# Thresholded attention and a gMLP on one core: the threshold taken as a sign bit on GpSimd and VectorE, one Exp per step, and q, k transposed by half tiles

## The chip, the cores and the metric

The kernel runs on one core of one Trainium2 chip. The metric is the device time of one execution in microseconds. The kernel before took 428.83 us, the median of three runs (428.46 to 429.54).

## The reference, cut to what matters

```python
scale = 1.0 / np.sqrt(64)                       # q, k, v: (8, 8, 576, 64)
scores = scale * (q @ k.T)
thresh = max(scores, axis=-1) - tau             # tau = 0.02
scores = where(scores >= thresh, scores, -1e9)
attn = softmax(scores)
x = (attn @ v) in the layout (8, 576, 512)      # heads side by side
h = relu(x @ w_in); u, v = halves of h          # w_in: 512 x 1024
v_n = layernorm(v)
v_s = w_spatial @ v_n + b_spatial               # w_spatial: 576 x 576
out = (u * v_s) @ w_out                         # w_out: 512 x 512
```

So every query row keeps only the keys whose score lies within tau of the row's largest, and a gated MLP follows for each of the 8 batches.

## The kernel before, in words

The attention is cut into 144 steps, 18 for each batch. A step `g` holds 128 queries of two heads of one pair against all 576 keys. These pieces belong to a step, each named by a letter in the order lists:

- `S`, `G`, `Y` (`scores`, `turn_bank`, `scores_end`, line 830): TensorE computes both heads' scores in fp32 into one of two PSUM rings `s`, in four 64x64 quarters of the array. `G` is an empty instruction on another engine that orders two writes to one bank.
- `M` (`top`, line 859): VectorE copies each head's 128x576 scores from PSUM to SBUF (`e`, a ring of 3) and finds the row maximum `peak` on the way. TensorE may write that `s` ring again only when `M` is done.
- `B` (`shift`, lines 869 and 873): 128x2 elements, `negm` from `peak`, on VectorE or GpSimd.
- `E`, `F` (`spread`, lines 887 and 890): ScalarE, once for each head. In the steps that the table `WAYS` marks `a` it is a Prelu with slope 1e30 below the threshold, and `Z` (`exps`, line 925) is then one Exp over both heads, 128x1152. In the 42 steps marked `n` it is an Exp to fp16, and VectorE then makes a mask (`C`, `keep`, line 909) and ands it in (`A`, `pick`, line 918).
- `T` (`turn_p`) transposes the numerators `p` by DMA into `pT`, and `P`, `i`, `p` (`product`) multiply them with v and normalise.

Besides, each pair of heads has its q and k transposed on TensorE. `QA` and `QB` (`qk_main`, line 448) are one block for q and one for k, four fp32 transposes of 128x128 each into one PSUM bank `f`, and `qa`, `qb` evict one bank each on ScalarE or VectorE (`evict`, lines 422 to 430); q is multiplied by the scale there. Two `f` banks serve all products and transposes that aren't scores.

The order of all work on every engine is written out by hand: `ORDER` has one list of tokens for each batch, `run_token` calls the piece that a token names, and each engine works through its own queue in that order. A `d` ahead of a token moves its eviction to VectorE; `a`, `g`, `v` ahead of `G` or `B` name the engine.

Of the kernel before, what the change touches and what calls it, by code (L numbers as in the profile page):

```python
# [34 lines left out]
(  # L35
# [18 lines left out]
(  # L54
# [117 lines left out]
(  # L172
# [1090 lines left out]
```

## Time and profile before

| | |
|---|---|
| median of the runs | 428.83 us |
| profiled execution, its own time | 429.39 us |
| its span | 427.6 us |
| busy: PE, DVE, ACT, POOL | 405.0, 384.0, 386.1, 191.4 us |
| TensorE clock | granted in full in all of the span |

PE is TensorE, DVE is VectorE, ACT is ScalarE, POOL is GpSimd. Busy time counts an engine's instructions from start to end, where two overlap once. A matmul's recorded end is modelled, so a busy PE isn't PE at its peak. Around the span lie 1.8 us of the profiled execution's own time, and the median is 0.6 us under that time.

### The profile page before, as it was taken

What the parts mean: (1) busy time and instruction counts of PE and PEld (TensorE: products, weight loads), DVE (VectorE), ACT (ScalarE), POOL (GpSimd) and SP (SyncE); (2) the same over time, 40 slices, a digit from 0 to 9 for tenths busy, and PEclk for the clock granted to TensorE, in tenths of its full rate; (3) what the DMA queues carried; (4) which work ended last, traced back from release to release, by engine and by line L of the source; (5) the groups of instructions that cost most, each with busy time, mean ns of one, the idle gap of its engine ahead of it and who ended that gap; (6) DMA issues with size and microseconds to landing.
All of it is one profiled execution on the core that took longest, in us unless ns stands there. A gap on an engine that the chain in (4) does not pass through costs nothing.

```text
span 427.6 us, 13266 instructions
## 1 busy us (share of the span) xinstructions
PE 405.0 (95%) x4978; PEld 253.3 (59%) x5029; DVE 384.0 (90%) x1035; ACT 386.1 (90%) x567; POOL 191.4 (45%) x469
## 2 busy tenths in 40 slices
PE   8778978999999999999999999999999999999995
PEld 4456655566555675575665657656665666565642
DVE  6999989999899899989999999989999989999562
ACT  4999979999999999999999999999999999999362
POOL 2566437763246633554235631374233753255020
PEclk9999999999999999999999999999999999999999
DMA  7999999999999999998999989999989999989913
GB/s 196 288 280 182 263 273 227 168 182 195 239 265 171 214 213 188 204 210 227 214 165 280 211 165 252 217 221 210 236 138 229 228 214 206 160 150 214 180 57 117
DMA packets 224703, 88.18 MB, mean 206 GB/s; under 512 B 195648, under 2 KB 220352, under 8 KB 224640
## 3 DMA queue, kind: packets, MB, share of 16 engines
q1 hardware_dynamic: 224192, 86.75, 102.3%
q8 instruction: 39, 0.64, 0.6%
q10 hardware_dynamic: 368, 0.33, 0.2%
q0 software_dynamic: 80, 0.26, 0.2%
q14 instruction: 24, 0.20, 0.2%
HBM read 32.79 MB, written 9.44 MB: 99 GB/s over the span
## 4 chain that ended last, share of the span: by engine, by line
PE 62%; DVE 11%; ACT 9%; DMA 7%; issue 5%; POOL 3%; SPq 1%; POOLq 0%; DVEq 0%; ACTq 0%
PE s L830 25%; DVE e L859 7%; PE f L752 6%; DMA pT<-p 6%; PE f L448 5%; PE f L510 5%; PE f L723 4%; PE f L656 4%; ACT e L890 3%; PE f L781 3%; ACT e L887 2%; PE f L505 2%; ACT p L925 1%; DMA xT<-xn 1%; PE f L641 1%
## 5 line engine op out<-in xcount | busy, mean ns | idle before, releaser
L859 DVE CUSTOM_DVE_ANT_0 e<-s,zero 128x576 f32<-128x576 f32 x288 | 204.3, 752 | 5.8 <-PE s L830 1.4
L830 PE MATMUL s<-qkT 64*64 64x160 f32 (+1 forms) x2304 | 172.9, 413 | 4.5 <-DVE peak L859 3.7
L890 ACT ACTIVATE e<-e,negm 128x576 f32<-128x576 f32 x204 | 148.3, 766 | 4.8 <-PE s L830 2.3
L830 PEld LDWEIGHTS s<-qkT 64*64 64x64 f32 x2304 | 105.3, 132 | 53.2 <-issue 19.1
L925 ACT ACTIVATE p<-e 128x1152 f16<-128x1152 f32 x102 | 117.1, 1157 | 0.8
L873 POOL TENSOR_SCALAR negm<-peak 128x2 f32<-128x2 f32 x93 | 21.5, 231 | 133.3 <-DVE peak L859 89.7
L887 ACT ACTIVATE e<-e,negm 128x576 f16<-128x576 f32 x84 | 62.4, 767 | 2.0 <-POOL negm L873 1.3
L510 PE MATMUL f<-v,pT 128*128 128x65 bf16 x984 | 44.6, 194 | 0.0
L510 PEld LDWEIGHTS <-pT 128*128 128x128 f16 x1024 | 41.9, 98 | 2.4 <-issue 0.6
L918 DVE TENSOR_TENSOR p<-e 128x576 int32<-128x576 int32 x42 | 34.4, 822 | 0.5
L752 PE MATMUL f<-wsT,vn 128*128 128x512 bf16 x121 | 31.9, 380 | 0.9 <-DVE qkT L424 0.2
L505 PE MATMUL f<-v,pT 128*128 128x130 bf16 x123 | 27.2, 221 | 4.0 <-DMA pT<-p 3.9
L333 POOL CAST v<-vl 128x512 bf16<-128x512 f32 x32 | 21.3, 666 | 18.6 <-PE s L830 17.5
L708 POOL TENSOR_SCALAR vn<-vrel,rs,nm 128x512 bf16<-128x512 f32 (+1 forms) x35 | 27.9, 798 | 3.6
L723 PE MATMUL f<-xT,w_in 128*128 128x512 bf16 x102 | 28.5, 380 | 1.0 <-ACT qkT L430 0.3
L656 PE MATMUL f<-w_in,xT 128*128 128x512 bf16 x98 | 27.0, 380 | 1.4 <-DMA xT<-xn 0.3
L548 DVE TENSOR_TENSOR xn<-f,r 128x384 bf16<-128x384 f32 x46 | 25.2, 554 | 0.7
L781 PE MATMUL f<-w_o,gT 128*128 128x512 bf16 x94 | 25.1, 379 | 0.4
L859 DVE DVE_READ_ACCUMULATOR2_ANT peak<- 128x1 f32 x288 | 23.9, 83 | 0.0
L306 POOL COPY qn<-ql 128x512 f32<-128x512 f32 x31 | 19.7, 636 | 5.9 <-DMA ql<-in_q_dram 2.7
L752 PEld LDWEIGHTS <-vn 128*128 128x128 bf16 x140 | 12.8, 98 | 15.5 <-issue 3.1
L448 PE MATMUL f<-identf,kn 128*128 128x128 f32 x124 | 19.8, 282 | 2.2 <-DVE qkT L424 1.5
(175 smaller groups left out, 560.2 us busy)
## 6 DMA issues: line engine op xcount, KB each, us to landing
vl<-in_v_dram SPq DMA_DIRECT2D x16, 512.0 KB, 5.2
ql<-in_q_dram SPq DMA_DIRECT2D x15, 512.0 KB, 5.5
kl<-in_k_dram SPq DMA_DIRECT2D x15, 512.0 KB, 5.7
out_dram<-oo SPq DMA_DIRECT2D x12, 512.0 KB, 4.2
pT<-p SPq DMA_TRANSPOSE x141, 4.4
uT<-in_moe_w_in_dram SPq DMA_DIRECT2D x3, 512.0 KB, 6.4
uT<-in_moe_w_spatial_dram SPq DMA_DIRECT2D x2, 576.0 KB, 6.8
vx<-in_v_dram SPq DMA_DIRECT2D x16, 64.0 KB, 3.8
```

The source lines that it names most:

```text
L448: nc.tensor.transpose(out=t[:, c * P:(c + 1) * P], in_=nat[i][which][:, c, :], identity=identf)
L505: nc.tensor.matmul(out=t[:, at:at + 130], lhsT=pt[:, 4, rows], rhs=vt[:, 4:6, :].rearrange("p b d -> p (b d)"), start=True, stop=False)
L510: nc.tensor.matmul(out=t[:, at + 65 * h:at + 65 * h + 65], lhsT=pt[:, 5 * h + j, rows], rhs=vt[:, 6 * h + j, :], start=False, stop=(h == 1 ...
L656: nc.tensor.matmul(out=t, lhsT=x_of(b, f, slice(c * P, (c + 1) * P)), rhs=w_in[:, f, 512:1024], start=(f == 0), stop=(f == 3))
L723: nc.tensor.matmul(out=t, lhsT=w_in[:, m, f * P:(f + 1) * P], rhs=x_of(b, m, slice(0, 512)), start=(m == 0), stop=(m == 3))
L752: nc.tensor.matmul(out=t, lhsT=vn[:, c, f * P:(f + 1) * P], rhs=wsT[:, c, 0:512], start=(c == 0), stop=(c == 4))
L781: nc.tensor.matmul(out=t[:n], lhsT=gs[b][:, f, c * P:c * P + n], rhs=w_o[:, f, :], start=(f == 0), stop=(f == 3))
L830: made.append(nc.tensor.matmul(out=s_ring[g % 2][halves[k], at[h] + lo:at[h] + hi], lhsT=qks[n][halves[h], 0, m:m + 64], rhs=qks[n][halves ...
L859: nc.vector.tensor_tensor_reduce(out=e_ring[g % 3][:, h, :], in0=view(s_ring[g % 2], at[h], [[1, S]]), in1=zero.broadcast_to([P, S]), scal ...
L887: nc.scalar.activation(out=half_e(g)[0][:, h, :], in_=s, func=ACT.Exp, bias=bias_, scale=scale if steps[g][1] == 4 else 1.0)
L890: nc.scalar.activation(out=e, in_=s, func=ACT.Prelu, bias=bias_, scale=scale if steps[g][1] == 4 else 1.0, alpha=1e30)
L925: nc.scalar.activation(out=numerators(g), in_=e_ring[g % 3].rearrange("p h s -> p (h s)"), func=ACT.Exp)
```

## The change: what it does

- **The threshold.** `M` now multiplies by the scale as it copies. `B` (`bound`) makes `low = tau - peak`. `E` and `F` (`spread`) are one add and one multiply, `(s + low) * 2^-126`, in place in `e`, for all 288 heads of steps: a kept score becomes a small positive fp32 whose bits, read as an int32, are `(s - peak + tau) * 2^23`, and every other one is negative and so a hugely negative int32. `Z` is one Exp over 128x1152 for every step, which reads `e` as int32, multiplies by 2^-23 and adds -tau. The ways, the masks and the `C`, `A` tokens are gone.
- **Where it runs.** `E` and `F` leave ScalarE: 154 of the 288 are on GpSimd and 134 on VectorE (the `d` tokens). `B` is 71 times on GpSimd and 73 times on VectorE, before 93 and 51. `Z` on ScalarE is 144 instead of 102.
- **q and k.** `QX` transposes q and k of a pair in one block of 16 transposes: each reads 64 rows of the array and writes 128x64, and they go in turn to the two halves of the rows and to the two `f` banks. `qx` and `qy` each evict a whole bank, with half of the columns of q and of k. The scale isn't applied there any more.
- **Rings.** `e` has 4 buffers instead of 3, `p` 9 instead of 10.
- **Lists.** All order lists are new. Evictions moved with them: of the 62 of q and k 8 are on VectorE (before 27) and 54 on ScalarE (before 35), and VectorE has 8 fewer of the 128x512 evictions of `uT` (11 before).

```diff
-    def qk_main(i, which):
+    def qk_main(i):
+        hold = []
         def mm():
-            t = hold["t"] = bank()
-            for c in range(4):
-                nc.tensor.transpose(out=t[:, c * P:(c + 1) * P], in_=nat[i][which][:, c, :],
-                                    identity=identf)
+            hold.extend(bank() for _ in range(2))
+            for c in range(8):
+                w, n = divmod(c, 4)
+                for r in range(2):
+                    nc.tensor.transpose(
+                        out=hold[r][:, 64 * c:64 * c + 64], in_=nat[i][w][halves[r], n, :],
+                        identity=identf[halves[r], halves[r]])
+        def ev(r):
+            dst = qk_of(i)[:, :, 64:S].rearrange("p w (c s) -> p w c s", c=4)
+            evict(dst[:, :, :, 64 * r:64 * r + 64],
+                  hold[r].rearrange("p (w c s) -> p w c s", w=2, c=4))
...
-                in1=zero.broadcast_to([P, S]), scale=1.0, scalar=float("-inf"),
+                in1=zero.broadcast_to([P, S]), scale=scale, scalar=float("-inf"),
...
+    def bound(g):
+        low[g] = small.tile([P, 2], F32, name="low")
+        (nc.vector if on_vector[0] else nc.gpsimd).tensor_scalar(
+            out=low[g], in0=peak[g], scalar1=-1.0, scalar2=tau, op0=ALU.mult, op1=ALU.add)
     def spread(g, h):
-        if way(g) in "nrs":
-            nc.scalar.activation(out=half_e(g)[0][:, h, :], in_=s, func=ACT.Exp,
-                                 bias=bias_, scale=scale if steps[g][1] == 4 else 1.0)
-        elif on_act(g):
-            nc.scalar.activation(out=e, in_=s, func=ACT.Prelu, bias=bias_,
-                                 scale=scale if steps[g][1] == 4 else 1.0, alpha=1e30)
+        e = e_ring[g % NE][:, h, :]
+        (nc.vector if on_vector[0] else nc.gpsimd).tensor_scalar(
+            out=e, in0=e, scalar1=low[g][:, h:h + 1], scalar2=2.0 ** (SHIFT - 149),
+            op0=ALU.add, op1=ALU.mult)
-    def keep(g):
...
-    def pick(g):
...
     def exps(g):
-        nc.scalar.activation(out=numerators(g), in_=e_ring[g % 3].rearrange("p h s -> p (h s)"),
-                             func=ACT.Exp)
+        nc.scalar.activation(out=numerators(g),
+                             in_=e_ring[g % NE].rearrange("p h s -> p (h s)").bitcast(I32),
+                             func=ACT.Exp, bias=wrap, scale=2.0 ** -SHIFT)
```

The rows below are the engines' queues in the order of the program. On VectorE, between the tops of steps 87 and 88 (batch 4), before:

```order
L545 RECIPROCAL r<-f_92 128x6
L548 TENSOR_TENSOR xn<-f_92,r 128x384
L909 TENSOR_SCALAR e_109<-e_109 128x2x576
L859 ISA e_108,peak<-s_96,zero 128x576
L859 ISA peak 128x1
L859 ISA e_108,peak<-s_96,zero 128x576
L859 ISA peak 128x1
L869 SCALAR_TENSOR_TENSOR negm<-peak,raised 128x2
L918 TENSOR_TENSOR p_116<-e_109 128x576
```

And after the change, at the same place (`e_106` to `e_109` are the four buffers of `e`):

```order
L848 TENSOR_SCALAR low<-peak 128x2 x2
L854 TENSOR_SCALAR e_108<-e_108,low 128x576
L667 BN_STATS st<-vrel 128x6
L671 BN_AGGR mv<-st 128x2
L854 TENSOR_SCALAR e_108<-e_108,low 128x576
L667 BN_STATS st<-vrel 128x6
L840 ISA e_106,peak<-s_96,zero 128x576
L840 ISA peak 128x1
L840 ISA e_106,peak<-s_96,zero 128x576
L840 ISA peak 128x1
```

The mask and the and of an `n` step (lines 909 and 918) are gone, and both heads' add and multiply of step 86 (line 854) stand between two tops, with their bounds (line 848) ahead of them on the same engine.

On GpSimd, behind the last normalised tile `vn` of batch 4's gMLP, before:

```order
L708 TENSOR_SCALAR vn_136<-vrel,rs,nm 128x512
L873 TENSOR_SCALAR negm<-peak 128x2
L306 COPY qn<-ql_138 128x512
L306 COPY kn<-kl_139 128x512
L460 COPY qkT<-qkT 64x64 x2
L873 TENSOR_SCALAR negm<-peak 128x2 x3
```

And after the change:

```order
L700 TENSOR_SCALAR vn_135<-vrel,rs,nm 128x512
L454 COPY qkT<-qkT 64x64
L854 TENSOR_SCALAR e_106<-e_106,low 128x576
L854 TENSOR_SCALAR e_107<-e_107,low 128x576 x2
L322 CAST v_131<-vl_139 128x2x4x64
L328 CAST v_131<-vx_145 64x64 x2
```

Three adds and multiplies of 128x576 stand where 128x2 shifts stood, and the copies that prepare the next pair's q, k and v (`qn`, `kn`, `v`) queue behind them.

On TensorE, where q and k of a pair are transposed behind scores (batch 3), before:

```order
L830 MATMUL s_97<-qkT 64x416 x4
L830 MATMUL s_97<-qkT 64x160 x2
L448 MATMUL f_91<-identf,qn 128x128 x4
L656 LDWEIGHTS xT
L656 MATMUL f_92<-w_in,xT 128x512
```

And after the change (the first rows of 16 transposes; scores follow the last):

```order
L812 MATMUL s_96<-qkT 64x160 x2
L812 MATMUL s_96<-qkT 64x416 x4
L812 MATMUL s_96<-qkT 64x160 x2
L442 MATMUL f_91<-identf,qn 128x64
L442 MATMUL f_92<-identf,qn 128x64
```

Before, a transposing block took one bank and a product took the other at once; now one block takes both banks in turn. In the whole queue scores and other work on TensorE change places 216 times before and 238 times after.

## Rows read from the trace of the kernel before

**Rows 1.** The page's head, and busy time, share and instructions of each engine.

```profile
span 427.6 us, 13266 instructions
PE 405.0 (95%) x4978; PEld 253.3 (59%) x5029; DVE 384.0 (90%) x1035; ACT 386.1 (90%) x567; POOL 191.4 (45%) x469
```

**Rows 2.** Busy time in two stretches: PE, PEld, DVE, ACT, POOL, clock, DMA.

```profile
20.00:396.00 376.00, 362.60 (x4544) 228.72 (x4586) 352.64 (x940) 359.63 (x521) 180.29 (x441) 1.00 1.08 212
396.00:427.60 31.60, 26.18 (x292) 14.99 (x292) 15.12 (x40) 13.31 (x26) 3.31 (x5) 1.00 0.49 117
```

**Rows 3.** The chain that ended last, its shares of the span by engine.

```profile
PE 62%; DVE 11%; ACT 9%; DMA 7%; issue 5%; POOL 3%; SPq 1%; POOLq 0%; DVEq 0%; ACTq 0%
```

**Rows 4.** VectorE's timeline near 150 us: start, length, instruction.

```profile
150.32 0.75 DVE L859 CUSTOM_DVE_ANT_0 e<-s,zero 128x576 f32<-128x576 f32 x1
...
151.67 0.69 DVE L766 TENSOR_TENSOR gT<-f,uT 128x512 bf16<-128x512 f32 x1
152.27 0.15 DVE L869 SCALAR_TENSOR_TENSOR negm<-peak,raised 128x2 f32<-128x2 f32 x1
```

**Rows 5.** VectorE's groups by shape: count, busy us, mean ns, idle before.

```profile
L918 DVE TENSOR_TENSOR p<-e 128x576 int32<-128x576 int32 x42 | 34.4, 822 | 0.5
L909 DVE TENSOR_SCALAR e<-e 128x1152 uint16<-128x1152 f16 x42 | 19.8, 474 | 1.3 <-ACT e L887 0.9
L869 DVE SCALAR_TENSOR_TENSOR negm<-peak,raised 128x2 f32<-128x2 f32 x51 | 10.3, 202 | 1.3 <-PE s L830 0.6
L420 DVE TENSOR_SCALAR uT<-f 128x512 bf16<-128x512 f32 x11 | 7.5, 681 | 0.8 <-PE f L723 0.8
L321 DVE COPY kn<-kl 128x512 f32<-128x512 f32 x1 | 0.4, 427 | 0.5 <-DMA kl<-in_k_dram 0.5
```

**Rows 6.** VectorE's timeline near 412 us, two scalings of 128x512 from SBUF.

```profile
412.36 0.55 DVE L970 TENSOR_SCALAR vn<-vrel,rstd,shift 128x512 bf16<-128x512 f32 x1
...
413.10 0.94 DVE L970 TENSOR_SCALAR vn<-vrel,rstd,shift 128x512 bf16<-128x512 f32 x1
```

**Rows 7.** GpSimd's timeline at the same place.

```profile
412.99 0.77 POOL L970 TENSOR_SCALAR vn<-vrel,rstd,shift 128x512 bf16<-128x512 f32 x1
```

**Rows 8.** Line 918 in the steady stretch: count, shortest, median and longest ns.

```profile
L918 DVE TENSOR_TENSOR p<-e x40: 725/758/1476, 21.0 to 395.7; 128x576 int32<-128x576 int32 x40
```

**Rows 9.** VectorE's timeline near 228 us.

```profile
228.38 1.14 DVE L918 TENSOR_TENSOR p<-e 128x576 int32<-128x576 int32 x1
```

**Rows 10.** GpSimd's timeline near 228 us.

```profile
228.29 0.61 POOL L306 COPY kn<-kl 128x512 f32<-128x512 f32 x1
```

**Rows 11.** GpSimd's groups by shape.

```profile
L708 POOL TENSOR_SCALAR vn<-vrel,rs,nm 128x512 bf16<-128x512 f32 x28 | 22.6, 807 | 2.9
L873 POOL TENSOR_SCALAR negm<-peak 128x2 f32<-128x2 f32 x93 | 21.5, 231 | 133.3 <-DVE peak L859 89.7 <-PE s L830 7.5 <-ACT e L890 6.8
```

**Rows 12.** ScalarE's groups by shape.

```profile
L890 ACT ACTIVATE e<-e,negm 128x576 f32<-128x576 f32 x204 | 148.3, 766 | 4.8 <-PE s L830 2.3 <-POOL negm L873 1.8
L925 ACT ACTIVATE p<-e 128x1152 f16<-128x1152 f32 x102 | 117.1, 1157 | 0.8
L428 ACT ACTIVATE qkT<-f 128x512 f32<-128x512 f32 x18 | 10.6, 589 | 3.4 <-PE f L448 3.4
```

**Rows 13.** Pieces of the chain near 224 us: start, length, line.

```profile
223.18 1.13 PE s L830 x12
224.31 0.59 PE f L448 x4
...
225.76 0.95 PE f L781 x4
226.71 0.45 PE f L448 x4
```

**Rows 14.** TensorE's timeline near 54 us.

```profile
54.13 0.42 PE L524 MATMUL f<-v,pT 128*64 128x65 bf16 x16
...
54.55 0.41 PE L510 MATMUL f<-v,pT 128*128 128x65 bf16 x8
```

More of the change, by code (lines that the diff above doesn't have):

```diff
@@ L1 @@
-import math
 from contextlib import ExitStack
@@ L13 @@
 I32 = mybir.dt.int32
-U16 = mybir.dt.uint16
 AX = mybir.AxisListType
@@ L214 @@
     P = 128
+    NE, NP = 4, 9
+    tau = min(float(tau), 128.0)
+    SHIFT = 23
+    while 2 * tau >= 2.0 ** (24 - SHIFT):
+        SHIFT -= 1
     const = ctx.enter_context(tc.tile_pool(name="const", bufs=1))
@@ L241 @@
     identh = const.tile([P, P], F16, name="identh")
-    ntau = const.tile([P, 1], F32, name="ntau")
-    ctau = const.tile([P, 1], F32, name="ctau")
+    wrap = const.tile([P, 1], F32, name="wrap")
+    used = const.tile([P, 1], F32, name="used")
     mhalf = const.tile([P, 1], F32, name="mhalf")
     zero = const.tile([P, 1], F32, name="zero")
-    raised = const.tile([P, 2, 2], F32, name="raised")
     warm = const.tile([P, P], BF16, name="warm")
-    e_ring = [const.tile([P, 2, S], F32, name=f"e{i}") for i in range(3)]
-    p_ring = [const.tile([P, 1152], F16, name=f"p{i}") for i in range(10)]
+    e_ring = [const.tile([P, 2, S], F32, name=f"e{i}") for i in range(NE)]
+    p_ring = [const.tile([P, 1152], F16, name=f"p{i}") for i in range(NP)]
     pT_ring = [const.tile([P, 9, P], F16, name=f"pT{i}") for i in range(12)]
@@ L434 @@
     rest_late = (0, 1, 2)
+    halves = [slice(64 * k, 64 * k + 64) for k in range(2)]
     def qk_of(i):
@@ L440, in qk_of @@
         return qks[i]
-    def qk_main(i, which):
-        hold = {}
+    def qk_main(i):
+        hold = []
         def mm():
-            t = hold["t"] = bank()
-            for c in range(4):
-                nc.tensor.transpose(out=t[:, c * P:(c + 1) * P], in_=nat[i][which][:, c, :],
-                                    identity=identf)
-        def ev():
-            if which == 0:
-                evict(qk_of(i)[:, 0, 64:S], hold["t"], mul=scale)
-            else:
-                evict(qk_of(i)[:, 1, 64:S], hold["t"])
-        return "act", mm, ev
+            hold.extend(bank() for _ in range(2))
[9 more added lines that the diff above has]
+                  hold[r].rearrange("p (w c s) -> p w c s", w=2, c=4))
+        return "act", mm, lambda: ev(0), lambda: ev(1)
     def rest_first(eng, t):
@@ L494, in first @@
         turn(tq, 0, 0, 0)
-        nc.scalar.mul(out=qkt[:, 0, 64:192], in_=tq[:, 0:P], mul=scale)
+        nc.scalar.copy(out=qkt[:, 0, 64:192], in_=tq[:, 0:P])
         for c in range(1, 4):
             turn(tm, P * (c - 1), 0, c)
-        nc.scalar.mul(out=qkt[:, 0, 192:576], in_=tm[:, 0:384], mul=scale)
-    halves = [slice(64 * k, 64 * k + 64) for k in range(2)]
+        nc.scalar.copy(out=qkt[:, 0, 192:576], in_=tm[:, 0:384])
     def weigh(t, at, pt, vt, rows=slice(0, P)):
@@ L804 @@
     at = (96, 864)
-    def way(g):
-        return WAYS[min(g // 18, len(WAYS) - 1)][g % 18]
-    def on_act(g):
-        return way(g) in "anrs"
-    half_step = math.log1p(-2.0 ** -12)
     def follow(b, a):
@@ L850, in scores_end, with top @@
         follow(part(g, 1, 0, S - cut)[0], turned[g])
-    negm, peak = {}, {}
-    def top(g, heads=slice(0, 2)):
-        if g not in peak:
-            peak[g] = small.tile([P, 2], F32, name="peak")
-        for h in range(heads.start, heads.stop):
+    peak, low = {}, {}
+    def top(g):
+        peak[g] = small.tile([P, 2], F32, name="peak")
+        for h in range(2):
             nc.vector.tensor_tensor_reduce(
-                out=e_ring[g % 3][:, h, :], in0=view(s_ring[g % 2], at[h], [[1, S]]),
-                in1=zero.broadcast_to([P, S]), scale=1.0, scalar=float("-inf"),
+                out=e_ring[g % NE][:, h, :], in0=view(s_ring[g % 2], at[h], [[1, S]]),
+                in1=zero.broadcast_to([P, S]), scale=scale, scalar=float("-inf"),
@@ L862, in top @@
                 op0=ALU.add, op1=ALU.max, accum_out=peak[g][:, h:h + 1])
-    def shift(g, engine):
-        nm = negm[g] = small.tile([P, 2], F32, name="negm")
-        down = -(scale if steps[g][1] == 4 else 1.0)
-        if engine is nc.vector:
-            engine.scalar_tensor_tensor(out=nm, in0=peak[g], scalar=down,
-                                        in1=raised[:, 0 if way(g) == "a" else 1, :],
-                                        op0=ALU.mult, op1=ALU.add)
-        else:
-            engine.tensor_scalar(out=nm, in0=peak[g], scalar1=down,
-                                 scalar2=float(tau) + (0.0 if way(g) == "a" else half_step),
-                                 op0=ALU.mult, op1=ALU.add)
@@ L895, in numerators @@
-    def numerators(g):
-        return p_ring[g % 10]
-    def mask(g):
-        ef = e_ring[g % 3].rearrange("p h s -> p (h s)")
-        nc.vector.scalar_tensor_tensor(out=numerators(g), in0=ef, scalar=ctau, in1=ef,
-                                       op0=ALU.is_ge, op1=ALU.mult)
-    def keep(g):
-        e, kept = half_e(g)
-        if way(g) == "n":
-            nc.vector.tensor_scalar(out=kept.bitcast(U16), in0=e, scalar1=1.0, scalar2=65535.0,
-                                    op0=ALU.is_ge, op1=ALU.mult)
-        else:
-            nc.vector.tensor_scalar(out=kept, in0=e, scalar1=1.0, scalar2=None, op0=ALU.is_ge)
@@ L928, in turn_p @@
     def turn_p(g):
-        nc.sync.dma_start_transpose(out=pT_ring[g % 12], in_=p_ring[g % 10])
+        nc.sync.dma_start_transpose(out=pT_ring[g % 12], in_=p_ring[g % NP])
     staged = []
@@ L1116, in run_token @@
         relay = nc.gpsimd
-        if name[0] in "agv" and name[1] in "GB":
+        if name[0] in "agv" and name[1] == "G":
             relay = {"a": nc.scalar, "g": nc.gpsimd, "v": nc.vector}[name[0]]
@@ L1123, in run_token @@
         kind = name.rstrip("0123456789")
-        a = [int(x) for x in name[len(kind):]] if kind not in "SGYMHKBEFZWCAT" else []
-        g = 18 * b + int(name[len(kind):]) if kind in "SGYMHKBEFZWCAT" else 0
+        a = [int(x) for x in name[len(kind):]] if kind not in "SGYMBEFZT" else []
+        g = 18 * b + int(name[len(kind):]) if kind in "SGYMBEFZT" else 0
         if b >= B or g >= len(steps):
-            return
-        if kind in stepwise and way(g) not in stepwise[kind]:
             return
@@ L1131, in run_token @@
         m = 2 * b + a[0] if a else 0
-        if kind in "SGYMHKEFBZWCAT":
-            {"S": scores, "G": lambda g: turn_bank(g, relay), "Y": scores_end, "M": top, "E": lambda g: spread(g, 0),
-             "F": lambda g: spread(g, 1), "H": lambda g: top(g, slice(0, 1)),
-             "K": lambda g: top(g, slice(1, 2)), "B": lambda g: shift(g, relay), "Z": exps, "W": mask, "C": keep, "A": pick, "T": turn_p}[kind](g)
-        elif kind in ("QA", "QB", "qa", "qb"):
-            task("q", i, kind[1] in "Bb")[1 + (kind[0] == "q")]()
+        if kind in "SGYMBEFZT":
+            {"S": scores, "G": lambda g: turn_bank(g, relay), "Y": scores_end, "M": top, "B": bound,
+             "E": lambda g: spread(g, 0), "F": lambda g: spread(g, 1), "Z": exps,
+             "T": turn_p}[kind](g)
+        elif kind in ("QX", "qx", "qy"):
+            task("q", i)[1 + ("QX", "qx", "qy").index(kind)]()
         elif kind in ("QR", "qr", "kd"):
@@ L1185 @@
         nc.vector.memset(zero, 0.0)
-        nc.gpsimd.memset(raised[:, 0], float(tau))
-        nc.gpsimd.memset(raised[:, 1], float(tau) + half_step)
-        nc.vector.memset(ntau, -float(tau))
+        nc.vector.memset(wrap, -float(tau))
         nc.vector.memset(mhalf, -0.5)
-        nc.scalar.activation(out=ctau, in_=ntau, func=ACT.Exp)
+        nc.scalar.activation(out=used, in_=wrap, func=ACT.Exp)
         nc.vector.tensor_copy(out=identb, in_=identf)
```

30 lines of the change are left out of this document (4 added, 26 removed), and 278 rows, old and new, of tables (LAST, ORDER).

## The prediction

> **What bounds the kernel now.** I read the busy times first, then a stretch without head and tail, then the chain of waits. TensorE, VectorE and ScalarE are busy for 405, 384 and 386 us of 427.6, GpSimd for 191 [rows 1]. Between 20 and 396 us, 376 us in all, they fill 362.6, 352.6 and 359.6 us, so 96, 94 and 96%, and GpSimd 180, 48% [rows 2]. Three engines are full at once; whichever is late holds up the other two, and no single one can be relieved with much effect. In the tail the same three are busy for 26, 15 and 13 of 31.6 us [rows 2]; the change leaves that stretch nearly as it is. The chain runs through TensorE for 62% of the span, VectorE 11%, ScalarE 9%, GpSimd 3% [rows 3]: some 265, 47, 38 and 13 us. So TensorE's own work sets most of the time, and ScalarE's 38 us are what can be won if it is never late.
>
> On VectorE an instruction costs less than its length, since the next starts ahead of its end. Two head passes of the top begin at 150.32 and the next operation at 151.67, 0.68 us each for a length of 0.75, and a product of 0.69 is followed after 0.60 [rows 4]. I take 0.08 us off every length there, and the same on ScalarE.
>
> **The change part by part: ScalarE.** It loses 288 activations at 0.766, 204 of that row and 84 of another form as long: 288 x 0.69 = 198 us. It gains 42 Exps of 1.157: 45 us. It gains 19 evictions of q and k, at 0.589, so 10 us, and an estimated 14 us of others that left VectorE [rows 12]. That makes 386 - 198 + 45 + 24 = some 257 us, 60% of the span. No row shows an Exp that reads int32. If it were half as long again, 144 x 0.58 = 83 us would come on top and ScalarE would still be at 340, under what it was; I take no difference.
>
> **VectorE.** It loses 42 masks at 0.474 and 42 ands at 0.822, so 16.5 + 31.2 us; 19 evictions of q and k and 8 of `uT` at 0.681, so 16.2; and 28 smaller evictions, for which I estimate 10. It gains 22 bounds at 0.202: 2.7 [rows 5]. That is 384 - 71 = 313 us. Then come 134 adds and multiplies of 128x576 fp32 in SBUF, which no row has. From below: the fp32 copy of 128x512 in SBUF takes 0.427 where the same size from PSUM takes 0.681, so it runs faster than one element at a time [rows 5]; 64 elements more add 0.03, less the overlap 0.38. From above: a scaling of 128x512 by two per-row numbers takes 0.55 when it runs alone [rows 6], so 0.50. One per-row number lies between: 0.44, in all 59 us (51 to 67). If it ran at one element a time, like the top, it would be 0.68 and 91 us.
>
> Then the two engines get in each other's way. The second such scaling takes 0.94 instead of 0.55, while GpSimd scales its own tile from 412.99 to 413.76 [rows 6, 7], and the and at 228.38 takes 1.14 instead of a median of 0.758, behind a GpSimd copy that ends at 228.90 [rows 8 to 10]. Both then end some 0.28 and 0.62 us after GpSimd does, so the later one waits for the earlier one's end and only its start-up is hidden. On average the ands lose 0.822 - 0.758 = 0.064 us each, with GpSimd busy for 45%. GpSimd will be busy for some 75% (below), in pieces a third longer: 0.064 x 1.67 x 1.33 = 0.14 us each, 19 us. From below, 0.05 and 7 us; from above half a GpSimd add of 0.84 in three of four cases, 0.31 and 42 us. So VectorE comes to 313 + 59 + 19 = 391 us, between 371 and 422: **no relief**, 7 us more than before by the middle.
>
> The Trainium skill says the same more strictly: its page "SBUF — State Buffer", section "Who interferes with whom", has VectorE in a two-port mode and GpSimd hold a shared port pair as a lock, where the second to issue blocks fully until the first is done. By that rule, with both halves of a step often ready at once, the upper price would hold; the rows agree that it blocks, but with the start-up hidden.
>
> **GpSimd.** It loses 22 bounds at 0.231, 5 us. 154 adds and multiplies come: from above the `vn` scaling, 0.807 for 512 elements and so 0.91 for 576 [rows 11]; from below the copy of 128x512 at 0.61, so 0.69 [rows 10]. The same kind of operation decides; part of it is fixed, as 128x2 takes 0.231 [rows 11], so 0.84: 129 us (106 to 140). With 10 us of waits for VectorE that is 191 - 5 + 129 + 10 = 325 us, and (180 + 134) / 376 = 84% of the steady stretch. It has its own queue to answer for now: the copies of the next q, k, v and the 128x2 bounds stand behind pieces of 0.84. What hides that is the ring of four `e` buffers, by which a top may run four steps ahead of its Exp, some 11 us at 2.9 us a step (427.6 / 144), while bound, two adds and Exp take 0.2 + 1.7 + 1.2 = 3.1. Without that cover each bound that waits 0.84 would hold up one top.
>
> **TensorE.** A block of four 128x128 transposes takes 0.45 us in the chain behind other work and 0.59 behind scores [rows 13], so 0.11 each and 0.14 for the change of layout. There are 31 x 8 of them, 27 us. Now 16 of half the rows and half the moving columns stand in for 8. From below, two run side by side and each takes half as long: 13.5 us. From above, nothing runs side by side and each load takes as long as before: 54. The nearest row has products in pairs of half the array's width: 16 in 0.42 us where 8 of full width take 0.41 [rows 14], so pairs do run side by side. But a half block still loads 128 columns, so I take 20, 7 us less. 22 more changes between scores and other work, at 0.14, give 3 back. `QX` needs both `f` banks empty at once; at worst each of 31 waits for a whole eviction of 0.59 [rows 12], 18 us, covered by the scores ahead of it. ScalarE, which does 54 of the 62, will be free to evict at once; I take 2. So TensorE: -2 us (-13 to +40).
>
> **The sum.** Along the chain: ScalarE's 38 us shrink. E and F leave it, and Z and the evictions find it idle four times in ten: I take 15 left, -23. GpSimd's 13 grow with its busy time, x 1.7: +9. VectorE's 47 grow by its 7 us of 384, and by 5 for the steps whose E and F stand in its queue ahead of a top: +6. TensorE -2. In all -10 us on the span of 427.6, so 417.6; with the 1.2 us by which the median lies over the span, **419 us**. Cross-check: VectorE's steady stretch of 352.6 + 7 would have to run 98% full to fit into 366 us. That is tight, and it is why I don't forecast more.
>
> **The rivals.** *(a) The port decides, slower.* For it: rows 6 to 10, and that both engines get 576-element pieces at the same moments. Against it: most steps are given whole to one engine, as in the rows of the order. At the upper price VectorE needs 23 us more than in my sum: 442. It decides from 0.14 + 10 / 134 = 0.21 us a piece on. *(b) Half tiles load one after the other*, slower: TensorE +34 against my sum, some of it under waits: 435 to 445. For it: nothing in the rows shows two row halves loading 128 fp32 columns. The Trainium skill's page "TensorE: Matmul & The Clock Gate", section "LDWEIGHTS (loading the stationary operand)", gives the load a time by its columns alone, columns / 1.2 in ns, so 107 ns whatever the rows: twice as many loads, and 27 us more by an estimate from that page, if they don't overlap. *(c) GpSimd is the bound*: from 1.13 us a piece on its steady stretch is as full as ScalarE's was; at 1.2 us, 435. Against it: 0.807 for the same kind. *(d) Nothing gained*: ScalarE's place in the chain goes to VectorE whole, 428 to 430. *(e) More gained*: the lower prices on VectorE, 371 us, 13 less than before; its steady 340 at 96% need 354 us, and the time is 404 to 411.
>
> **How the numbers follow.** My forecast (411 to 427) 0.46, (e) 0.22, (d) 0.08, (a) 0.13, (b) 0.06, (c) 0.05. 0.3% is 1.3 us, about what a measurement of this kernel can tell from no change. Faster: 0.46 + 0.22 = 0.68; same 0.08; slower 0.24. The range reaches from 405 to 434: it leaves out the lowest part of (e), some 0.05, and the larger part of (a) to (c), some 0.15.
>
> **What would show it.** ScalarE near 257 us busy and gone from the chain's first places; line 854 at some 0.52 on VectorE when alone (0.44 + 0.08) with a tail up to 1.2, and at 0.84 on GpSimd; VectorE at 380 to 400 busy; GpSimd above 310; the 16 transposes of a `QX` in some 0.65 us plus the change of layout. The forecast is wrong if line 854's mean on VectorE is over 0.75, if a `QX` takes over 1 us, if GpSimd's queue shows up ahead of tops or transposes in the waits, or if TensorE's own order of work holds it where ScalarE did.

## The result: 434.78 us, 1.0% slower

The changed kernel takes 434.78 us, median of 4 runs (431.06 to 437.43), the kernel before 429.19 on the same chip: a ratio of 1.010, 95% interval 1.0055 to 1.0145. The forecast was 419 us and faster, with a range from 405 to 434. The ratio, here and in the table below, is estimated from single fast executions, while the times are medians of all, which stand 1.3% apart here. The profiled execution took 434.25 us.

The page of the changed kernel, head, busy times and the chain's shares, answers to [rows 1, 3]:

```profile
span 432.4 us, 13715 instructions
PE 403.8 (93%) x5226; PEld 246.0 (57%) x5277; DVE 383.3 (89%) x1052; ACT 283.1 (65%) x376; POOL 306.3 (71%) x599
...
PE 64%; DVE 19%; DMA 6%; issue 4%; ACT 4%; SPq 2%; POOL 0%; DVEq 0%; ACTq 0%; POOLq 0%
```

ScalarE lost 103 us of work and nearly left the chain, as announced. VectorE's load stayed as it was, and it took ScalarE's place: 19% of 432.4 is 82 us, before 47. GpSimd's share fell from 3% to 0, though it is busy for 306 us instead of 191, and TensorE's rose from some 265 to 277 us. Two stretches of windows answer to [rows 2] (columns as there):

```profile
20.00:400.00 380.00, 361.69 (x4785) 221.51 (x4829) 351.05 (x956) 261.25 (x340) 293.44 (x568) 0.99 1.07 208
400.00:432.40 32.40, 27.50 (x299) 15.67 (x302) 16.39 (x44) 14.48 (x27) 3.34 (x6) 1.00 0.49 114
```

TensorE and VectorE fill 95 and 92% of the stretch, nearly as before. The prices of single pieces, by shape (count, busy us, mean ns, idle before), and of line 854 also the shortest, median and longest ns:

```profile
L854 DVE TENSOR_SCALAR e<-e,low 128x576 f32<-128x576 f32 x134 | 77.6, 599 | 2.5 <-PE s L812 2.1
L864 ACT ACTIVATE p<-e,wrap 128x1152 f16<-128x1152 int32 x144 | 178.6, 1254 | 56.4 <-POOL e L854 24.0 <-DVE e L854 19.4 <-DMA pT<-p 5.3
L442 PE MATMUL f<-identf,qn 64*128 64x64 f32 x248 | 16.3, 239 | 0.5 <-DVE gT L758 0.2
L442 PE MATMUL f<-identf,kn 64*128 64x64 f32 x248 | 13.3, 224 | 0.0
...
L854 POOL TENSOR_SCALAR e<-e,low x154: 739/745/1298, 13.1 to 399.3; 128x576 f32<-128x576 f32 x154
L854 DVE TENSOR_SCALAR e<-e,low x134: 470/516/1295, 10.8 to 401.3; 128x576 f32<-128x576 f32 x134
```

A `QX` in the chain; one weight load of 64 rows after and of 128 rows before (shortest, median, longest ns); the scores after and before:

```profile
223.49 0.64 PE f L442 x16
...
L442 PEld LDWEIGHTS f<-identf,qn x248: 134/138/223, 10.7 to 384.7; 64*128 64x128 f32 x124
L448 PEld LDWEIGHTS f<-identf,qn x124: 137/141/146, 8.2 to 374.1; 128*128 128x128 f32 x124
...
L812 PE MATMUL s<-qkT 64*64 64x416 f32 (+1 forms) x2304 | 181.1, 417 | 10.1 <-DVE peak L840 7.4
L830 PE MATMUL s<-qkT 64*64 64x160 f32 (+1 forms) x2304 | 172.9, 413 | 4.5 <-DVE peak L859 3.7
```

From its first start to its last end the median `QX` takes 0.71 us. But the scores keep TensorE busy for 8.2 us more than before.

The longest piece of line 854 on VectorE, and what GpSimd did:

```profile
83.11 1.11 POOL L371 CAST wsb<-uT 128x512 bf16<-128x512 f32 x1
83.25 1.29 DVE L854 TENSOR_SCALAR e<-e,low 128x576 f32<-128x576 f32 x1
```

It ends 0.32 us after GpSimd's copy. 35 of the 134 pieces take over 0.6 us, and all 35 end 0.31 to 0.32 us after an instruction on GpSimd does; the 14 that meet nothing on GpSimd take 0.48 to 0.52.

**Where the time went.** Set side by side, top by top, the changed kernel is up to 4.2 us later and up to 5.0 us earlier on the way. At step 132 the two are level, and step 138 starts 6.3 us later than before (after and before, each time):

```profile
361.69 0.76 DVE L840 CUSTOM_DVE_ANT_0 e<-s,zero 128x576 f32<-128x576 f32 x1
360.94 0.75 DVE L859 CUSTOM_DVE_ANT_0 e<-s,zero 128x576 f32<-128x576 f32 x1
...
385.91 0.75 DVE L840 CUSTOM_DVE_ANT_0 e<-s,zero 128x576 f32<-128x576 f32 x1
379.65 0.76 DVE L859 CUSTOM_DVE_ANT_0 e<-s,zero 128x576 f32<-128x576 f32 x1 [0.76 <-POOL rs L701]
```

So in the profiled execution the loss arises between the two. The chain between the two, in order of time (start, length, what):

```profile
364.54 0.28 PE f L461
364.81 0.02 issue
364.84 0.30 DVE qkT L413
365.14 0.43 SPq L561
365.57 0.05 issue
365.62 5.35 DMA xT<-xn
370.97 0.05 issue
371.02 0.40 PE f L648
```

TensorE stands before the product of x with w_in (line 648) until a DMA transpose of x lands, which was issued late. Three windows of 4 us, one of them at the start, show TensorE's busy time (second number) and its granted clock (third from the end):

```profile
20.00:24.00 4.00, 4.00 (x47) 2.34 (x44) 3.02 (x8) 2.29 (x5) 3.67 (x7) 0.61 1.16 203
368.00:372.00 4.00, 1.59 (x18) 0.88 (x16) 3.05 (x8) 2.01 (x3) 3.68 (x9) 0.91 1.32 143
372.00:376.00 4.00, 4.00 (x30) 1.95 (x32) 1.74 (x4) 2.15 (x3) 1.79 (x5) 0.67 0.45 101
```

It is busy for 1.59 of 4 us, and around the end of that the clock is granted at its lower level, 1.2 GHz, for part of two windows: (0.09 + 0.33) x 4 = 1.7 us lost at most, by an estimate. The same happens at 20 us, 0.39 x 4 = 1.6 us, behind a stretch in which TensorE had waited for VectorE. In the profiled execution before it ran at 2.4 GHz there.

### The profile page after: what moved, and what is told of

It is laid out like the page before. It is cut to its first block, busy times and chain, and to the rows that moved or that the text cites. A ratio compares the mean times of both kernels' runs of the same rounds, so it can differ in the third digit from the quotient of the medians.

```text
span 432.4 us, 13715 instructions
## 1 busy us (share of the span) xinstructions
PE 403.8 (93%) x5226; PEld 246.0 (57%) x5277; DVE 383.3 (89%) x1052; ACT 283.1 (65%) x376; POOL 306.3 (71%) x599
## 4 chain that ended last, share of the span: by engine, by line
PE 64%; DVE 19%; DMA 6%; issue 4%; ACT 4%; SPq 2%; POOL 0%; DVEq 0%; ACTq 0%; POOLq 0%
PE s L812 26%; DVE e L840 10%; PE f L502 5%; DMA pT<-p 5%; PE f L715 5%; PE f L648 4%; PE f L744 4%; DVE e L854 4%; PE f L773 3%; PE f L442 3%; ACT p L864 2%; PE f L497 2%; SPq L870 2%; PE f L633 2%; DVE gT L758 1%
## 5 line engine op out<-in xcount | busy, mean ns | idle before, releaser
L864 ACT ACTIVATE p<-e,wrap 128x1152 f16<-128x1152 int32 x144 | 178.6, 1254 | 56.4 <-POOL e L854 24.0
L812 PE MATMUL s<-qkT 64*64 64x416 f32 (+1 forms) x2304 | 181.1, 417 | 10.1 <-DVE peak L840 7.4
L854 POOL TENSOR_SCALAR e<-e,low 128x576 f32<-128x576 f32 x154 | 120.0, 779 | 26.9 <-DVE low L848 5.0
L854 DVE TENSOR_SCALAR e<-e,low 128x576 f32<-128x576 f32 x134 | 77.6, 599 | 2.5 <-PE s L812 2.1
L419 ACT COPY qkT<-f 128x512 f32<-128x512 f32 (+1 forms) x78 | 35.8, 487 | 29.8 <-PE f L442 16.4
L744 PE MATMUL f<-wsT,vn 128*128 128x512 bf16 x126 | 31.0, 379 | 1.1 <-DVE qkT L413 0.7
L648 PE MATMUL f<-w_in,xT 128*128 128x512 bf16 x103 | 28.2, 394 | 2.4 <-DMA xT<-xn 1.5
L848 POOL TENSOR_SCALAR low<-peak 128x2 f32<-128x2 f32 x71 | 15.4, 217 | 20.3 <-DVE peak L840 13.7
L660 ACT ACTIVATE vrel<-f 128x512 f32<-128x512 f32 (+1 forms) x28 | 16.5, 594 | 11.5 <-PE f L648 7.4
```

Source lines behind the costliest of these rows:

```text
L419: nc.scalar.copy(out=out, in_=in_)
L648: nc.tensor.matmul(out=t, lhsT=x_of(b, f, slice(c * P, (c + 1) * P)), rhs=w_in[:, f, 512:1024], start=(f == 0), stop=(f == 3))
L744: nc.tensor.matmul(out=t, lhsT=vn[:, c, f * P:(f + 1) * P], rhs=wsT[:, c, 0:512], start=(c == 0), stop=(c == 4))
L812: made.append(nc.tensor.matmul(out=s_ring[g % 2][halves[k], at[h] + lo:at[h] + hi], lhsT=qks[n][halves[h], 0, m:m + 64], rhs=qks[n][halves ...
L854: (nc.vector if on_vector[0] else nc.gpsimd).tensor_scalar(out=e, in0=e, scalar1=low[g][:, h:h + 1], scalar2=2.0 ** (SHIFT - 149), op0=ALU ...
L864: nc.scalar.activation(out=numerators(g), in_=e_ring[g % NE].rearrange("p h s -> p (h s)").bitcast(I32), func=ACT.Exp, bias=wrap, scale=2. ...
```

## The experiments

Ratios are to the kernel before on the same chip; the changed kernel's own is 1.010. The runs e2, e5, e6, e8, e11 and e13 to e16 leave work out and compute something else: they ask what that work costs. The diffs are abridged.

| run | us | ratio, interval |
|---|---|---|
| e1 full tiles | 436.78 | 1.0158 (1.0129 to 1.0187) |
| e2 no pieces on VectorE | 425.96 | 0.9918 (0.9882 to 0.9953) |
| e3 35 steps on ScalarE | 460.61 | 1.0721 (1.0687 to 1.0756) |
| e4 x earlier | 431.58 | 1.0039 (1.0016 to 1.0063) |
| e5 before, no E and F | 427.36 | 0.9923 (0.9893 to 0.9953) |
| e6 no pieces at all | 423.07 | 0.9809 (0.9756 to 0.9861) |
| e7 before, half tiles | 489.29 | 1.1344 (1.1301 to 1.1388) |
| e8 less TensorE | 429.89 | 0.9981 (0.995 to 1.0013) |
| e9 evictions to ScalarE | 453.01 | 1.0535 (1.0496 to 1.0573) |
| e10 statistics too | 477.71 | 1.1097 (1.1056 to 1.1138) |
| e11 e6 and e8 | 420.50 | 0.9792 (0.974 to 0.9844) |
| e12 relays to ScalarE | 456.74 | 1.0617 (1.0571 to 1.0664) |
| e13 short transposes | 432.93 | 1.0079 (1.0051 to 1.0107) |
| e14 before, the same | 425.31 | 0.9893 (0.9861 to 0.9926) |
| e15 e11 and e13 | 408.18 | 0.9492 (0.9459 to 0.9526) |
| e16 no late loads | 432.44 | 1.0078 (1.0051 to 1.0104) |
| e17 step 1 on ScalarE | 429.61 | 1.0002 (0.9962 to 1.0042) |
| e18 top 4 first | 430.66 | 1.0012 (0.9977 to 1.0048) |

### What was ScalarE worth? (e5)

```diff
 def spread(g, h):
+    return
```

> The kernel before without its 288 activations of line 890 and 887 on ScalarE (the two E and F of a step; left out and not moved, and the tops add a constant, so that what the later operations read is finite): 288 x 0.766 = 221 us off ScalarE, 386 to 165. It asks what ScalarE was worth in the kernel before. Theory G (TensorE was the bound: in the steady 376 us it was idle for 13.4 us in all, so no more can be won there): 418 to 426 us. The prediction's step (ScalarE's 38 us of the chain can be won): 406 us or less.

The diff leaves out two constants that keep the numbers finite. Measured: 427.36 us against 430.87, so 3.5 us less, over 1 us above theory G's range and 21 above the most that the prediction's step allows. The run's busy times and its chain:

```profile
PE 406.1 (95%) x4978; PEld 255.3 (60%) x5029; DVE 382.6 (90%) x1035; ACT 199.6 (47%) x279; POOL 192.7 (45%) x469
...
PE 74%; DVE 9%; DMA 7%; issue 4%; SPq 1%; POOL 1%; ACT 1%; DVEq 0%; POOLq 0%; ACTq 0%
```

ScalarE has 186 us less to do, and its share of the chain falls from 9% [rows 3] to 1%, some 38 to 4 us. The time falls by a tenth of that. TensorE's share grows from 62 to 74%: what ScalarE ended before, TensorE's work now fills. This settles the forecast's main term as far as the kernel before goes.

### VectorE, GpSimd, TensorE, one by one (e2, e6, e8, e11)

```diff
 def spread(g, h):                       # e2; in e6 a bare return
+    if by_vector[g, h]:
+        return
-            for f in range(4):           # e8, lines 648 and 715
+            for f in range(2):
```

> The changed kernel without the 134 adds and multiplies that stand on VectorE (77.6 us busy there); they are left out and not moved, so those rows of the softmax are not thresholded, and the Exp of such a step reads the same integers with a scale 256 times smaller, at the same size and type. Theory A (VectorE full): VectorE falls to about 305 us busy, TensorE gets its maxima sooner, and the time falls to 400 to 415 us, where TensorE (403.8 us busy) is the bound. Rival C (GpSimd's pieces come late and hold ScalarE's Exp: 24.0 us of ScalarE's idle time was ended by GpSimd's line 854): the late pieces are still there, 425 to 433 us. Rival D (TensorE's own order holds it whatever the others do): 432 to 436 us.

> The changed kernel without all 288 adds and multiplies, on VectorE and on GpSimd (left out; nothing is thresholded, the Exp reads the same integers with a scale 256 times smaller): VectorE falls to about 305 us busy, GpSimd to about 185. Without VectorE's share alone it took 425.96 us. Theory G (TensorE's own 398 to 404 us of work, its start and its tail are the floor): 418 to 424 us. Rival C (GpSimd's late pieces held the run without VectorE's share): 410 us or less.

> The changed kernel with half of TensorE's work left out in two places: the products of x with w_in sum over two of the four blocks of 128 (lines 648 and 715, steady part alone), so that 27.7 of the 403.8 us of TensorE go and no other engine has less to do. Theory G (TensorE is the bound): 20 to 28 us less than the changed kernel, 407 to 415 us. Theory A (VectorE is the bound, busy 383 us): 428 to 434 us.

> The changed kernel with both reliefs at once: no adds and multiplies at all (423.07 us alone), and half of the products of x with w_in left out (429.89 us alone). Theory H (two bounds close together: TensorE's work with start and tail gives some 423, VectorE's some 428): with both lowered the time falls by more than the 12 and 5 us add up to, to 395 to 408 us. Rival D (the order of the lists and the latencies between engines hold it): 415 to 420 us.

Busy times of e2, e6, e8 and e11, in this order:

```profile
PE 398.0 (94%) x5226; PEld 244.0 (58%) x5277; DVE 321.0 (76%) x918; ACT 281.9 (67%) x376; POOL 286.9 (68%) x599
```

```profile
PE 398.0 (94%) x5226; PEld 244.0 (58%) x5277; DVE 316.8 (75%) x918; ACT 280.5 (66%) x376; POOL 170.6 (40%) x445
```

```profile
PE 383.5 (90%) x5112; PEld 233.6 (55%) x5157; DVE 383.3 (90%) x1052; ACT 280.9 (66%) x376; POOL 308.7 (72%) x599
```

```profile
PE 378.4 (91%) x5112; PEld 232.4 (56%) x5157; DVE 316.8 (76%) x918; ACT 279.1 (67%) x376; POOL 170.4 (41%) x445
```

VectorE with 62 us less gives 1.8% (0.9918 / 1.010), and GpSimd's pieces 1.1% more; TensorE with 20 us less gives 1.2%. None was the bound alone, so e2 missed its 400 to 415. It fell into rival C's range, but e6, without GpSimd's late pieces too, refutes C's 410 or less. Theory G (TensorE as the floor) has e6 right and misses e8 by 15 us, where theory A's 428 to 434 holds. Then I held TensorE and VectorE to be two bounds close together, and e11 was to show it at 395 to 408 us. It came to 420.5: that theory fell as well. With TensorE, VectorE and GpSimd lightened something else still held it, near rival D's 415 to 420.

### The DMA engines (e13 to e16)

```diff
-    dma_start_transpose(out=pT_ring[g % 12], in_=p_ring[g % NP])
+    k = 9 if g < 12 else 5               # e13, e14, e15
+    dma_start_transpose(out=pT_ring[g % 12][:, 0:k], in_=p_ring[g % NP][:, 0:k * P])
     elif kind == "L":                    # e16
+        if b < 2:
             load_of[b][a[0]]()
```

> The changed kernel with shorter DMA transposes of p: from the twelfth step on only five of the nine blocks are turned, the other four of a slot keep what an earlier step left there. No engine has less to do, the DMA engines some 17 of 88 MB and over a third of their packets. Theory K (the DMA engines are the bound that all runs share: the queue's packets take 101 to 104% of the span in every run from 417 to 432 us, 1.08 in the steady part): the time falls by 6 us or more, to 428 us or less, where TensorE (about 423) and VectorE (about 428) take over. Theory D (the order of the lists and the latencies from engine to engine): 432 to 436 us, or 1 to 3 us less since a transpose lands earlier.

> The same edit in the kernel before (five of nine blocks of p turned from the twelfth step on). Theory K: the kernel before ran on the DMA engines too, so 424 us or less. Theory D: 428 to 430 us.

> The changed kernel with all three reliefs: no adds and multiplies, half of the products of x with w_in, and the short transposes. The first two together took 420.5 us. Theory K: with the DMA engines relieved the time falls far below what the two gave, to 385 to 405 us. Theory D: 415 to 420 us.

> The changed kernel without the loads of q, k and v from the third batch on (their tiles keep the second batch's numbers): about 21 of 88 MB less on the same queue, in long packets, and the transposes of p as they are. Theory K: less, 424 to 430 us, by as much of the packets' time as the loads have. Theory D: 432 to 436 us.

The steady windows of e13 and of e15; the last column but one is the share of the 16 DMA engines, 1.07 in the changed kernel:

```profile
20.00:400.00 380.00, 363.90 (x4790) 223.21 (x4837) 351.46 (x958) 262.43 (x341) 295.12 (x568) 0.99 0.80 165
```

```profile
20.00:380.00 360.00, 341.18 (x4793) 212.98 (x4828) 290.35 (x837) 259.24 (x342) 160.85 (x417) 1.00 0.86 175
```

The DMA share falls by a quarter and the changed kernel gains 0.2%, within its interval. Fewer loads give as little. So the DMA engines alone aren't its bound: in e13 and e16 theory K missed and theory D's 432 to 436 holds. In the kernel before the same edit gives 1.1%, 425.31 us, between what the two theories had said. And on top of e11 the short transposes give 3%, 420.5 to 408.2, again between the two. The likely reading, not shown step by step, is that TensorE, VectorE with GpSimd, and the DMA engines are each filled so far that lightening one uncovers the next.

### Moving work to the engine with time left (e3, e9, e10, e12)

```diff
 def spread(g, h):                       # e3: the 35 steps with both heads on VectorE
+    if by_vector[g, 0] and by_vector[g, 1]:
+        nc.scalar.activation(out=e, in_=e, func=ACT.Prelu, bias=low[g][:, h:h + 1], alpha=1e30)
+        return
-dqy2:0 dqr3:0 deu2:1 deo1:2 ...         # e9: 29 evictions on ScalarE, with e4
+qy2:0 qr3:0 eu2:1 eo1:2 ...
-bv3:1 bs3:1 ba3:1                       # e10: with e9
+ev3:1 n3:1 k3:1
-vG5:0                                   # e12: with e9, 47 tokens
+aG5:0
```

> The changed kernel with the adds and multiplies of the 35 steps that have both heads on VectorE (70 of 134) taken by ScalarE, as a Prelu with slope 1e30 below zero and the low bound as its bias, and a plain fp32 Exp in those steps, as the kernel before had it. By the rows VectorE loses 70 x 0.599 = 42 us (383 to 341) and ScalarE gains 70 x 0.766 - 35 x 0.097 = 50 us (283 to 333), still less than the 386 us that it had before. Theory A: 415 to 426 us, faster than both kernels. Rival C or D (GpSimd late, or TensorE's order): no gain, 430 to 437 us. Rival E: ScalarE's evictions now wait behind the new pieces, 436 to 445 us.

> The kernel with x earlier (431.58 us), and the evictions from PSUM that the lists give to VectorE given to ScalarE, each at its place: by the rows 8 x 0.686, 5 x 0.683, 3 x 0.679, 7 x 0.288 and some smaller, about 14 us off VectorE (384 to 370), and about 12 us onto ScalarE (283 to 295). Theory H (TensorE and VectorE are two bounds close together, and what comes off VectorE alone is worth about a ninth, as 77.6 us less gave 8.8): 429 to 431 us. Rival E (an eviction on ScalarE stands behind an Exp that waits for GpSimd's piece): 433 us or more.

> The same, and the statistics of vrel that VectorE made (22 of 128 rows and 6 of 64, 0.68 + 0.17 us each) made by ScalarE and GpSimd in the kernel's other way: a sum with the Relu, a mean on GpSimd, a Square with a sum on ScalarE. About 24 us more off VectorE (370 to 346), some 26 us onto ScalarE (295 to 321), 28 small pieces of 0.2 onto GpSimd. Theory H: 426 to 429 us, so faster than before. Rival E: 433 us or more.

> The kernel of the run with evictions on ScalarE, and the 47 empty instructions that pass on the release of a score bank in VectorE's queue put into ScalarE's queue at the same place. In the changed kernel with x earlier TensorE waited 5.5 us for VectorE's queue there, in five waits, and 1.6 us for ScalarE's 73 in six. Theory H: 2 to 4 us less than without this edit, 426 to 429 us. Rival E (ScalarE's queue stands behind Exps that wait for GpSimd): no less, or more.

All four lose 21 to 46 us, e3 against the changed kernel and the others against e4, though VectorE has less to do. Rival E's direction is what came each time, in e3 well beyond its 436 to 445. ScalarE's groups and VectorE's waits for ScalarE in e3:

```profile
L884 ACT ACTIVATE p<-e,wrap 128x1152 f16<-128x1152 int32 x109 | 135.1, 1252 | 31.7 <-POOL e L870 19.3 <-DVE e L870 6.4 <-issue 3.4
L881 ACT ACTIVATE p<-e 128x1152 f16<-128x1152 f32 x35 | 40.7, 1164 | 0.9 <-PE s L812 0.7
...
DVE e L852 <- ACT p L884: 15.6, 10, 2.9
DVE e L852 <- ACT p L881: 9.7, 10, 2.1
```

The tops waited 1.7 us for `p` in the changed kernel and wait 25 us here. A step with two pieces on ScalarE holds it for 2 x 0.770 + 1.164 = 2.7 us in a row, and the `e` ring of four fills. In e9 VectorE's tops wait for the scores instead:

```profile
DVE e L840 <- PE s L812: 20.1, 27, 4.6
```

6.1 us in e4. And TensorE's waits that ScalarE ends, mostly by an eviction, add up to some 30 us in e9 and 10 in e4: TensorE needs the bank. ScalarE is idle for a third of the time, but at its place in the queue an eviction can stand behind an Exp that waits for GpSimd's or VectorE's piece (24.0 and 19.4 us of such waits above); that this is what delays the evictions is argued, not shown. In these lists ScalarE's idle time couldn't be used; no run tried a new order. What e10 and e12 add is open.

### Half tiles (e1, e7)

```diff
-for c in range(8): ... for r in range(2): transpose(64 rows, out=hold[r][:, 64 * c:64 * c + 64])
+for w in range(2): ... for n in range(4): transpose(128 rows, out=hold[w][:, P * n:P * n + P])
```

> The changed kernel with q and k of a head pair turned by full 128x128 tiles again, q into one bank and k into the other, each copied out whole; everything else, and every place in the lists, as changed. Theory A (VectorE is still the full engine: 383 us busy after, 384 before, 36 to 38 of every 40 us): the half tiles cost or save TensorE about what the prediction said, 2 to 4 us over the kernel, and TensorE mostly waits for VectorE, so the time stays at 432 to 437 us. Rival B (the half tiles are what cost: their sixteen transposes and two banks at once hold TensorE): 425 to 430 us, and the 16-transposes-a-pair of lines 442 give way to a shorter stay at that place.

> The kernel before with the half tiles alone: q and k of a pair turned together in 16 half tiles, q unscaled and the scale put into the activations and the bound; the lists differ only in where these tokens stand (pairs 5 and 9 eight and ten places earlier, the others within six). By full tiles in the changed kernel (412.7 us of busy TensorE against 403.8, and 436.8 us against 434.8) half tiles save TensorE some 9 us busy and the kernel some 2 us. Theory G: 425 to 428 us, faster than both. Rival B: half tiles cost, 431 us or more.

TensorE's transposes with full tiles in e1:

```profile
L441 PE MATMUL f<-identf,qn 128*128 128x128 f32 x124 | 20.5, 288 | 0.0
L441 PE MATMUL f<-identf,kn 128*128 128x128 f32 x124 | 18.6, 273 | 0.1
```

39.1 us busy against 29.6 with half tiles. Full tiles are 0.6% slower, so rival B, by which they would be faster, is out; the intervals just overlap, and the gain isn't shown more exactly. e7, the reverse edit in the kernel before, missed its 425 to 428 and lost 58 us. It can't be held against half tiles: its tokens moved too, and its lists now hold both banks at places made for one. What costs the 58 us stays open.

### The late x, and the start (e4, e17, e18)

```diff
-M6:0 P100:1 P101:1 P102:1 B6:0 ... i10:1 p10:1 T2:0 X1:1 X0:1 sv0:0
+P122:1 P100:1 P101:1 P102:1 i12:1 p12:1 i10:1 p10:1 X1:1 X0:1 s2:2 ... M6:0 B6:0 ... T2:0 sv0:0
+if g == 1: Prelu on ScalarE                              # e17, with e4
-kd1:0 dF3:0 S4:0 F2:0 ... dE1:0 dE2:0 E3:0 G4:0 Y4:0 M4:0    # e18, with e17
+kd1:0 S4:0 F2:0 ... dE1:0 E3:0 G4:0 Y4:0 M4:0 dE2:0 dF3:0
```

> The changed kernel with one place of the last list changed: the three products P100 to P102 of the batch before and their scaling stand right behind P120 to P122, and the two DMA transposes of x of that batch are issued right behind them, ahead of the p transpose of step 2. Theory F (5 to 6 us of the loss arise where TensorE stands idle for this x near 370 us, with the granted clock at half for 3.4 us behind it): 428 to 431 us, no idle stretch of over 1 us near 370 us and no half clock there. Rival A alone (VectorE is behind and the loss only shows there): 433 to 436 us, the start of step 138 as late as now.

> The kernel with x earlier (431.58 us), and the adds and multiplies of step 1 alone, two of four that stand in a row on VectorE ahead of the top of step 4 (3.02 us from 13.46 on, while TensorE stands idle for 2.02 us and ScalarE for 1.7), taken by ScalarE as a Prelu with a plain Exp behind it. Theory L (the rest of the loss is VectorE's row of pieces at the start): VectorE 1.5 us earlier at the top of step 4, TensorE's wait there halved, 429.5 to 431 us. Theory D (ScalarE's place in the order): the Exp of step 1 comes later, so no gain, or a loss as with the 35 steps.

> The same, and the top of step 4 ahead of the two other pieces of that row (E of step 2 and F of step 3). Theory L: TensorE's wait of 2.02 us at 16 us goes whole, the half clock behind it too, 428 to 430 us, so level with before or just under it. Theory D: the Exps of steps 2 and 3 come 1.5 us later and hold the tops of steps 6 and 7 by the ring of four: no gain.

The windows of e4 around the place:

```profile
368.00:372.00 4.00, 3.21 (x29) 1.60 (x27) 3.36 (x10) 2.68 (x5) 3.70 (x9) 1.00 1.17 182
372.00:376.00 4.00, 3.95 (x44) 2.29 (x44) 3.56 (x9) 2.75 (x6) 2.96 (x6) 1.00 0.56 126
```

TensorE is busy for 3.21 us there instead of 1.59, the clock is whole, and step 138 starts 2.4 us earlier. The kernel takes 431.58 us, 0.6 above theory F's range: 1.0039 instead of 1.010, so over half of the loss by the middles of two intervals that just overlap. e17 and e18 are level with the kernel before (1.0002 and 1.0012), but their intervals overlap with e4's as well. And that e17 lies in its forecast range is luck: its reason isn't the one I gave. VectorE near 14 us in e17:

```profile
14.35 1.51 DVE L870 TENSOR_SCALAR e<-e,low 128x576 f32<-128x576 f32 x2 [0.31 <-POOL low L860]
16.56 0.76 DVE L852 CUSTOM_DVE_ANT_0 e<-s,zero 128x576 f32<-128x576 f32 x1 [0.70 <-ACT e L867]
```

The top of step 4 starts at 16.56, in e4 at 16.41: the row of pieces is shorter, but now the top waits for ScalarE and the ring. What e17's trace lacks is a stretch at the lower clock, which e4 has near 36 us (0.83 and 0.74 from 32 to 40). Whether the edit or the execution decides that is left open, since the kernel before has mean granted clocks down to 0.991 in its executions beside e17 too. e18 missed by 0.7 us, and its clock falls to 0.60 from 20 to 24 us, which theory L had excluded.

## Why the prediction was wrong

- **The failed step** is the first term of the sum: "ScalarE's 38 us are what can be won if it is never late", taken as -23, and with it the adding up of shares of the chain. The share did fall so (38 to 17 us), but e5 shows what that is worth: there it falls to 4 us, and 3.5 us are won. What ScalarE had ended, other engines then ended, TensorE in e5 and VectorE in the changed kernel. The rows held a warning: TensorE was idle for 376 - 362.6 = 13.4 us of the steady stretch [rows 2], less than the 23, though more than the 10 of the whole sum. The prediction itself noted that no single engine can be relieved with much effect, and that VectorE would have to run 98% full.
- **VectorE, +6.** Its share of the chain grew by 35 us. Its load was forecast as no relief, rightly: 383.3 us, below the 391. That is partly luck: by e2 the 134 pieces cost it 62 us instead of 78, and without them it is busy for 321 us instead of 313. Rival (d), ScalarE's place goes to VectorE whole, names what happened; its 428 to 430 us is under the measured time, and e17, without the late x and with another start, takes 429.61.
- **GpSimd, +9.** The term let its 13 us grow with its busy time. The busy time grew to 1.6 times what it was, but the share went to nothing: ScalarE's Exp waited for GpSimd for 24.0 us, and those waits didn't end the chain.
- **Prices.** Line 854 on VectorE: median 0.516 as announced (0.52), and a mean of 0.599, so 0.083 for the port instead of 0.14. On GpSimd 0.745 instead of 0.84, 120.0 us instead of 129; the prediction's own working (0.231 fixed, the rest by length) would have given 0.88. Rivals (a) and (c) needed 0.21 and 1.13 us and are refuted. The Trainium skill's page "SBUF — State Buffer", section "Who interferes with whom", has the later of the two engines blocked fully. The trace agrees that it waits, but the 35 long pieces end 0.31 us after GpSimd does where one alone takes 0.516, so some 0.2 us of the later one is hidden, as the prediction read from rows 6 to 10.
- **ScalarE, 257 us.** 283: an Exp that reads int32, with a bias and a scale, takes 1.254 us, not 1.157, 14 us in all; I had taken no difference. The other 12 are in what left: without `E` and `F` it loses 186 us in e5, where I had 198. It hardly cost time, if e5 may be carried over.
- **TensorE, -2.** The transposes cost 29.6 us busy, 39.1 with full tiles (e1), so 9.5 less, where the sum had 7; a `QX` takes 0.71 us (1.03 and more only in 5 of 31), where 0.65 and a change of layout were announced. Rival (b) is refuted by e1. The Trainium skill's page "TensorE: Matmul & The Clock Gate", section "LDWEIGHTS (loading the stationary operand)", prices a load by its columns alone; the trace agrees for one load (0.138 us for 64 rows, 0.141 for 128). By an estimate from that page twice as many loads would have cost 27 us more if none overlapped, and none of that shows: 16 of them fit into 0.71 us. What the sum lacked is on the other side: TensorE's busy time fell by 1.2 us only, since the scores took 181.1 us instead of 172.9, and its share of the chain grew by 12. Some 2 us of that may be the lower clock (178.8 in e17, whose trace has none up to its tail); no run separates the rest.
- **What no step had**: the new lists. One x is made and turned too late in the last list, and by e4 that is over half of the loss.

So most prices came out, and adding them up along the chain is what failed.

What isn't settled: which order would turn ScalarE's 150 idle us into time, and how much of the 1.0% is TensorE's clock. The four executions of the changed kernel had mean granted clocks of 0.982 to 0.996, and the fastest, 431.06 us, had the 0.996. No version that does the whole work beat the kernel before by more than its interval.

## What to carry to other kernels

A share of the chain of waits says who ended the waits, not what is won when he is faster: first take the idle time of the fullest engine in that stretch as a rough ceiling (13.4 us here, of which e5 won 3.5), and ask who ends the same waits next. Where several engines and the DMA engines are over 90% full, relief of one paid little and relief of all paid most (0.2 to 1.8% each here, 6% together). In a kernel with orders written by hand, a piece moved to an idle engine is a change of order, and that can cost more than the piece does: in e9 evictions of some 14 us cost 21.
